# K loads from the fifth on issued by ScalarE instead of SyncE, in a grouped-query softmax attention kernel

## The chip, the cores and the metric

The kernel runs on one core of a Trainium2 chip. The core has TensorE (PE; PEld is its weight load), VectorE (DVE), ScalarE (ACT), GpSimd (POOL) and SyncE (SP), each with its own instruction stream, and 16 DMA engines that all transfers share. A DMA is started by an instruction in the stream of some engine and is carried out behind its back; its landing is told by a semaphore. The metric is the device time of one launch in microseconds (us).

## The reference

Attention without a mask, where four query heads share one head of K and V:

```python
B, Hq, Hkv, Sq, Sk, D = 16, 32, 8, 16, 2048, 128     # all bf16
scores = jnp.einsum("bhqd,bhkd->bhqk", q, k) * D ** -0.5   # k, v repeated 4 times along h
p = jax.nn.softmax(scores, axis=-1)
return jnp.einsum("bhqk,bhkd->bhqd", p, v)
```

There are 16 x 8 = 128 groups (one head of K and V each). A group has 4 x 16 = 64 query rows, 2048 keys, 512 KB of K and 512 KB of V. K and V together are 134 MB, each byte of which is used once.

## The kernel before

Two groups make a pair (128 query rows); there are NP = 64 pairs, called p. V is loaded a pair at a time (1 MB, into one of NV = 8 buffers). K is loaded two pairs at a time (2 MB, 32 loads, into one of NK = 3 buffers): K load n serves the pairs 2n and 2n+1. In HBM a partition's share is one run of 16 KB in a K load and two runs of 4 KB in a V load.

For every K load VectorE works two steps, one for each half of the keys. Step s = 2n + x handles half x of the keys for both pairs of load n:

- VectorE transposes the half of K into KT (line 562, two instructions, "kt" below), two steps ahead of its use. Each of the two adds 1 to the semaphore `sem_kt`, so a K load is used up when four have been added.
- TensorE multiplies it with the turned queries into S_ps (lines 376 and 406).
- VectorE scales S_ps into Sneg and keeps the row minimum (line 573); after the second half it forms the bias of the pairs' exponentials (line 582).

ScalarE then takes the exponential of one pair (line 674, into one of two P buffers). TensorE turns P (line 414), ScalarE copies it to SBUF (line 683), TensorE multiplies with V ("PV", lines 429, 483 and 489), and ScalarE, for the last five pairs VectorE, divides by the row sum (lines 697, 701, 655: "norm"). PV(p) waits for V load p; it runs in the round of exponential p + 4. GpSimd lays out the queries.

The order on TensorE and ScalarE is written out by hand (`pe_prog`, `act_prog`). ScalarE's order in a round p of the main loop is: norm of p - 4, exponential of p, two copies of pair p - 2, and, where p is even, a copy of turned queries (line 664). An exponential waits for the transposes of P of pair p - 2 (the buffer is shared), one of an even pair also for the bias.

All DMAs are issued by SyncE in one loop over t, which also sets their order:

```python
for t in range(NP + SLAG + 1):
    ...                                   # Q loads at fixed t
    if t < NP and t % 2 == 0:
        load_k(t // 2)                    # waits: sem_kt >= 4 * (n - NK) + 4
    if 0 <= t - VLAG < VLATE:
        load_v(t - VLAG)                  # waits: PV(p - 8) done
    if VLATE <= t - VLAG - 1 < NP:
        load_v(t - VLAG - 1)
    if 0 <= t - SLAG < NP:
        store(t - SLAG)                   # waits: norm of that pair done
```

With VLAG = 6 and SLAG = 14, K load n is followed by V load 2n - 6, the store of pair 2n - 14, V load 2n - 5 and the store of pair 2n - 13. From V load 50 on (VLATE) V stands one t later. SyncE handles these in order: a wait in front of K holds the V loads and stores behind it too. K load n waits until the transposes of K load n - 3 are done, since it goes into the same buffer.

Of the kernel before, what the change touches and what calls it, by code (L numbers as in the profile page):

```python
# [11 lines left out]
NK = 3  # L12
# [21 lines left out]
VBASE = 16  # L34
HEAD = 40
RING = 6
VLOOP = (3, 30)
VHEAD = 140
EXPBASE = 3
# [5 lines left out]
def both_heads(p, NP):  # L45
    return p < NP - NFAST and p % 2 == 0


def bass_standalone__gqa_softmax__sampling_kernel(
# [11 lines left out]
    NP = G // 2  # L61
    NQD = NP // 2
# [11 lines left out]
    Kn = [sb(f"Kn{i}", [128, 4 * J * 128], BF16) for i in range(NK)]  # L74
# [10 lines left out]
    Osb = [sb(f"O{i}", [128, 128], BF16) for i in range(NO)]  # L85
    nhalf = sb("nhalf", [128, 2, RING], F32)
    nbias = sb("nbias", [128, RING], F32)
    rowsum = sb("rowsum", [128, RING], F32)
    rrec = sb("rrec", [128, RING], F32)

    def col(x, p):
        return x[:, p % RING:p % RING + 1]

    def pair(x, Q):
        return x[:, 2 * Q % RING:2 * Q % RING + 2]

    def o_done(p):
        return sem_o[p // NOG % (NO // NOG)], 16 * NOG * (p // NO)
# [12 lines left out]
    sem_k = [sem(f"sem_k{i}") for i in range(NK)]  # L111
# [4 lines left out]
    sem_kt = sem("sem_kt")  # L116
# [19 lines left out]
    kf = k.rearrange("b h s d -> (b h s d)").rearrange("(n a x) -> n a x", n=NQD, a=128)  # L136
# [20 lines left out]
    def pt_slot(p):  # L157
        return p % 2 if p < 2 * M1 - 2 else p % NPT
# [75 lines left out]
    def stage_ap(op):  # L234
        return ST_ps[:, 512 * stage_of[op]:512 * (stage_of[op] + 1)]
# [4 lines left out]
    def o_ap(p):  # L240
        if p < NP - 4:
            return O_ps[:, 0:128]
        x = p - (NP - 4)
        return S_ps[:, 512 * x:512 * x + 128]
# [4 lines left out]
    def lay_part(eng, k):  # L249
# [4 lines left out]
        region = i if c < 2 else 0  # L254
        return eng.tensor_tensor(Q4[:, region, :, :, :], src, by, op=ALU.mult)  # L255

    with nc.Block() as block:

        @block.gpsimd
# [49 lines left out]

        @block.sync  # L310
        def _(sp):
            def load_k(n):
                s = n % NK
                if n >= NK:
                    sp.wait_ge(sem_kt, 4 * (n - NK) + 4)
                sp.dma_start(Kn[s][:, :], kf[n]).then_inc(sem_k[s], 16)  # L316

            def load_v(p):
                s = p % NV
                if p >= NV:  # L320
                    sp.wait_ge(sem_pv, p - NV + 1)
                if p < NP - 1:
                    dst = Vb[:, s, :, :, :].rearrange("a g j d -> a g (j d)")
                    sp.dma_start(dst, vf[:, 2 * p:2 * p + 2, :]).then_inc(sem_v[s], 16)
                    return
                for x, (lo, hi) in enumerate(LASTV):
                    dst = Vb[:, s, :, lo:hi, :].rearrange("a g j d -> a g (j d)")
                    src = vf[:, 2 * p:2 * p + 2, 128 * lo:128 * hi]
                    sp.dma_start(dst, src).then_inc(sem_vl[x], 16)

            def load_q(c):
                s = c % NQ
                if c >= NQ:
                    if c == 2:
                        sp.wait_ge(sem_qa, 4)
                    elif c == 3:
                        sp.wait_ge(sem_qb, 4)
                    else:
                        sp.wait_ge(sem_q4, Q4BASE + 4 * (c - NQ) - 4)
                src = qf[1024 * c:1024 * (c + 1), :].rearrange("(a j) d -> a j d", j=8)  # L340
                sp.dma_start(Qn[s][:, :, :], src).then_inc(sem_q[s], 16)

            def store(p):
                s = p % NO
                if p < NP - NLATE:
                    sp.wait_ge(sem_nm, NMBASE + p + 1)
                else:
                    sp.wait_ge(sem_nl, p - (NP - NLATE) + 1)
                sp.dma_start(of[128 * p:128 * (p + 1), :], Osb[s][:, :]).then_inc(o_done(p)[0], 16)  # L349

            for t in range(NP + SLAG + 1):
                if t == 4:
                    for s in range(NV):
                        sp.sem_inc(sem_v[s], VBASE)
                    sp.sem_inc(sem_nm, NMBASE)
                    sp.sem_inc(sem_exp, EXPBASE)
                for c in range(NQC):
                    if t == (QLOAD[c] if c < len(QLOAD) else 8 * c - QLEAD):
                        load_q(c)
                if t < NP and t % 2 == 0:  # L360
                    load_k(t // 2)
                if 0 <= t - VLAG < VLATE:
                    load_v(t - VLAG)
                if VLATE <= t - VLAG - 1 < NP:
                    load_v(t - VLAG - 1)
                if 0 <= t - SLAG < NP:
                    store(t - SLAG)
            for g in range(NO // NOG):
                sp.wait_ge(sem_o[g], 16 * NOG * len(range(g, NP // NOG, NO // NOG)))
# [187 lines left out]
        def _(dve):  # L557
            def kt(n, e, k_at=None):
                Q, x = divmod(n, 2)
                if x == 0 and e == 0:  # L560
                    dve.wait_ge(sem_k[Q % NK], 16 * (Q // NK + 1) if k_at is None else k_at)
                dve.transpose(  # L562
                    KT[n % NKT][:, :].rearrange("p (t b g e a) -> p e g t b a", t=J // 4, b=2, g=4, e=2)[:, e],
                    Kn[Q % NK][:, :].bitcast(F32).rearrange(
                        "p (g x t e b c) -> p x e g t b c", g=4, x=2, e=2, b=2, c=32)[:, x, e],
                ).then_inc(sem_kt, 1)
# [42 lines left out]
            for n in range(2):  # L609
                for e in range(2):  # L610
                    kt(n, e)
            V0, V1 = VLOOP
            assert (V1 - V0) % 3 == 0 and V0 % 3 == 0 and V1 < NQD
# [43 lines left out]
        @block.scalar  # L657
        def _(act):
            for op in act_prog:
                if op[0] == "qe":  # L660
                    k = op[1]
                    c, i = divmod(k, 4)
                    act.wait_ge(sem_stq, k + 1)
                    act.activation(  # L664
                        QT[c % 2][:, i // 2, :].rearrange("p (a x j) -> p x a j", x=2, j=4)[:, i % 2],
                        stage_ap(("Q", k)).rearrange("p (j a) -> p a j", j=4), ACT.Copy,
                    ).then_inc(sem_qe, 1)
                elif op[0] == "exp":
                    _, p = op
                    if p % 2 == 0:  # L670
                        act.wait_ge(sem_nb, p // 2 + 1)
                    if p >= 2 and (p % 2 == 1 or p <= 2 * M1 + 2):
                        act.wait_ge(sem_pt, 2 * p - 2)
                    act.activation(  # L674
                        P[p % 2][:, :].bitcast(BF16),
                        Sneg[p % NS][:, :], ACT.Exp,
                        bias=col(nbias, p), scale=-1.0, accum_out=col(rowsum, p),
                    ).then_inc(sem_exp, 1)
                elif op[0] == "pe":
                    _, p, h = op  # L680
                    act.wait_ge(sem_pt, 2 * p + h + 1)
                    slot = pt_slot(p)
                    act.activation(  # L683
                        PT[slot][:, 4 * h:4 * (h + 1), :].rearrange("p t q -> p (t q)"),
                        stage_ap(("PT", p, h)), ACT.Copy,
                    ).then_inc(sem_ev[h], 1 + (EVBASE if p == 0 else 0))
                else:
                    _, p = op
                    if p % 2 == 0 and (p < 2 * M1 - 4 or p == NP - NLATE - 1):
                        act.wait_ge(sem_rec, p // 2 + 1)  # L690
                    if p >= NO and p % NOG == 0:
                        act.wait_ge(*o_done(p))
                    act.wait_ge(sem_pv, p + 1)
                    if both_heads(p, NP):
                        for g in range(2):
                            rows = slice(64 * g, 64 * (g + 1))
                            ins = act.activation(Osb[p % NO][rows, :], O_ps[rows, 128 * g:128 * (g + 1)], ACT.Copy,  # L697
                                                 scale=col(rrec, p)[rows])
                        ins.then_inc(sem_nm, 1)
                        continue  # L700
                    act.activation(Osb[p % NO][:, :], o_ap(p), ACT.Copy,  # L701
                                   scale=col(rrec, p)).then_inc(sem_nm, 1)
# [28 lines left out]
```

## Time and profile before

| | |
|---|---|
| median of 3 runs | 339.35 us (338.94 to 339.59) |
| the profiled execution | 338.73 us |
| its span, first to last instruction | 336.9 us |
| busy share: PE, DVE, ACT, POOL | 89%, 90%, 73%, 21% |
| DMA | 138.60 MB, mean 411 GB/s |
| K loads, issue to landing (median) | 18.6 us |
| V loads, issue to landing (median) | 16.9 us |
| granted TensorE clock | 0.995 |

Busy shares are averages over the whole span. A wait names the instruction that ended it. "SPq" is SyncE's instruction queue: its DMA instructions are not work of an engine, but each takes time in the queue, and the next must wait for it. The time from issue to landing holds the time that a transfer stands behind others.

### The profile page before, as it was taken

How to read it: one execution, taken by the hardware profiler on the slowest of the kernel's cores; microseconds unless marked ns; L12 is line 12 of the kernel's file. 1: busy time of each engine (PE TensorE's matmuls, PEld its weight loads, DVE VectorE, ACT ScalarE, POOL GpSimd, SP SyncE). 2: the span in 40 equal slices, each digit the busy share in tenths (PEclk: the TensorE clock that was granted, in tenths of full speed). 3: DMA queues.
4: the chain of work that ended last, by engine and by line, in shares of the span. 5: the costliest groups of instructions: out<-in, count | busy, mean ns of one | idle time of the engine just before them, and what ended most of it. 6: DMA issues, size and time to landing. Idle time of an engine off the chain costs nothing.

```text
span 336.9 us, 7946 instructions
## 1 busy us (share of the span) xinstructions
PE 299.8 (89%) x3264; PEld 172.9 (51%) x2752; DVE 304.7 (90%) x457; ACT 245.9 (73%) x376; POOL 69.7 (21%) x64
## 2 busy tenths in 40 slices
PE   3466899999999999999998998889898879999885
PEld 3012456655566555665555456455465445555564
DVE  1788999999999999999998999989899999999941
ACT  3124887888888898888876877767867787877873
POOL 2802022221222222222122222022221200000000
PEclk9998999999999999999999999999999999999999
DMA  7999999999999999999999999999999999999996
GB/s 294 443 413 431 414 410 408 418 424 426 420 413 413 423 424 422 417 411 421 426 427 416 410 417 424 425 418 422 409 422 425 430 416 424 418 411 416 413 412 226
DMA packets 32670, 138.60 MB, mean 411 GB/s; under 512 B 10896, under 2 KB 11152, under 8 KB 28560
## 3 DMA queue, kind: packets, MB, share of 16 engines
q1 hardware_dynamic: 32656, 138.42, 100.6%
q8 instruction: 8, 0.13, 0.2%
q14 instruction: 6, 0.05, 0.0%
HBM read 136.31 MB, written 2.10 MB: 411 GB/s over the span
## 4 chain that ended last, share of the span: by engine, by line
DMA 39%; PE 32%; DVE 21%; ACT 3%; issue 2%; SPq 2%; DVEq 0%; ACTq 0%
DMA Kn<-in_k_dram 25%; DMA Vb<-in_v_dram 14%; DVE Sneg L573 11%; DVE KT L562 10%; PE O_ps L429 9%; PE S_ps L406 8%; PE S_ps L376 7%; PE ST_ps L414 6%; PE ST_ps L392 2%; ACT P L674 1%; SPq L349 1%; ACT PT L683 1%; ACT QT L664 0%; PE S_ps L489 0%; SPq L316 0%
## 5 line engine op out<-in xcount | busy, mean ns | idle before, releaser
L562 DVE STREAM_TRANSPOSE KT<-Kn 128x1024 f32<-128x1024 f32 x128 | 151.0, 1219 | 9.0 <-DMA Kn<-in_k_dram 9.0
L573 DVE TENSOR_SCALAR_CACHE_REDUCE Sneg<-S_ps 128x1024 f32<-128x1024 f32 x128 | 150.1, 1207 | 8.5 <-PE S_ps L376 8.4
L674 ACT ACTIVATE P<-Sneg,nbias 128x2048 bf16<-128x2048 f32 x64 | 128.1, 2002 | 31.7 <-DVE nbias L582 15.7
L255 POOL TENSOR_TENSOR Q<-Qn,mask 128x1024 bf16<-128x1024 bf16 x28 | 52.9, 1894 | 135.4 <-PE ST_ps L392 128.9
L429 PE MATMUL O_ps<-Vb,PT 128*64 (+1 forms) x1104 | 68.8, 238 | 11.3 <-DMA Vb<-in_v_dram 10.2
L406 PE MATMUL S_ps<-KT,Q 64*128 64x512 bf16 x384 | 74.8, 386 | 0.0
L376 PE MATMUL S_ps<-KT,Q 64*128 64x512 bf16 x384 | 74.2, 383 | 0.0
L429 PEld LDWEIGHTS O_ps<-Vb,PT 128*64 128x64 bf16 (+1 forms) x1104 | 55.6, 106 | 35.2 <-issue 27.9
L683 ACT ACTIVATE PT<-ST_ps 128x512 f32<-128x512 f32 x128 | 68.8, 590 | 3.0 <-PE ST_ps L414 2.2
L414 PE MATMUL ST_ps<-ident,P 128*128 128x128 f32 x512 | 68.2, 276 | 1.5 <-ACT PT L683 1.2
L414 PEld LDWEIGHTS ST_ps<-ident,P 128*128 128x128 f32 x512 | 56.3, 141 | 5.9 <-ACT P L674 2.2
L697 ACT ACTIVATE O<-O_ps,rrec 64x128 bf16<-64x128 f32 x56 | 20.3, 362 | 38.2 <-PE O_ps L429 30.9
L406 PEld LDWEIGHTS S_ps<-KT,Q 64*128 64x128 bf16 x384 | 18.6, 93 | 49.7 <-issue 38.2
L406 PE MATMUL S_ps<-KT,QT 64*128 64x512 bf16 x128 | 28.2, 423 | 13.5 <-DVE Sneg L573 9.8
L392 PEld LDWEIGHTS ST_ps<-ident,Q 128*128 128x128 f32 x128 | 15.2, 153 | 25.4 <-issue 25.4
L376 PE MATMUL S_ps<-KT,QT 64*128 64x512 bf16 x128 | 28.2, 422 | 0.0
L392 PE MATMUL ST_ps<-ident,Q 128*128 128x128 f32 x128 | 22.2, 306 | 6.6 <-DVE Q L605 5.4
L294 POOL COPY Q<-QT 128x512 int32<-128x512 int32 x24 | 14.6, 610 | 58.8 <-PE S_ps L376 58.8
L664 ACT ACTIVATE QT<-ST_ps 128x512 f32<-128x512 f32 x32 | 19.3, 603 | 9.8 <-PE ST_ps L392 9.8
L406 PEld LDWEIGHTS S_ps<-KT,QT 64*128 64x128 bf16 x128 | 7.7, 99 | 34.1 <-issue 29.5
L701 ACT ACTIVATE O<-O_ps,rrec 128x128 bf16<-128x128 f32 x31 | 11.7, 378 | 2.4 <-PE O_ps L489 2.3
L674 ACT ACTIVATION_READ_ACCUMULATOR P<-Sneg,nbias 128x1 f32 x64 | 12.0, 188 | 0.0
(25 smaller groups left out, 71.6 us busy)
## 6 DMA issues: line engine op xcount, KB each, us to landing
Kn<-in_k_dram SPq DMA_DIRECT2D x32, 2048.0 KB, 18.6
Vb<-in_v_dram SPq DMA_DIRECT2D x63, 1024.0 KB, 16.9
Qn<-in_q_dram SPq DMA_DIRECT2D x8, 256.0 KB, 14.7
out_dram<-O SPq DMA_DIRECT2D x64, 32.0 KB, 16.1
Vb<-in_v_dram SPq DMA_DIRECT2D x1, 768.0 KB, 12.8
Vb<-in_v_dram SPq DMA_DIRECT2D x1, 256.0 KB, 12.5
```

The source lines that it names most:

```text
L255: return eng.tensor_tensor(Q4[:, region, :, :, :], src, by, op=ALU.mult)
L376: return pe.add_instruction(mybir.InstMatmult(name=nc.get_next_instruction_name(), engine=mybir.EngineType.PE, ins=[pe.lower_ap(rhs), pe.l ...
L392: ins = pe.transpose(dst[:, 128 * j:128 * (j + 1)], src[:, j, :], ident4[:, :])
L406: ins = pe.matmul(s_ap, w, x, start=(acc == 0), stop=(acc == 3))
L414: ins = pe.transpose(dst[:, 128 * t:128 * (t + 1)], ptile[:, 128 * x:128 * (x + 1)], ident4[:, :])
L429: return pe.add_instruction(mybir.InstMatmult(name=nc.get_next_instruction_name(), engine=mybir.EngineType.PE, ins=[x, pe.lower_ap(w, for_ ...
L562: dve.transpose(KT[n % NKT][:, :].rearrange("p (t b g e a) -> p e g t b a", t=J // 4, b=2, g=4, e=2)[:, e], Kn[Q % NK][:, :].bitcast(F32). ...
L573: ins = dve.tensor_scalar(Sneg[p % NS][:, 1024 * x:1024 * (x + 1)].rearrange("p (t a m) -> p t a m", t=4, m=8), S_ps[:, 1024 * y:1024 * (y ...
L664: act.activation(QT[c % 2][:, i // 2, :].rearrange("p (a x j) -> p x a j", x=2, j=4)[:, i % 2], stage_ap(("Q", k)).rearrange("p (j a) -> p ...
L674: act.activation(P[p % 2][:, :].bitcast(BF16), Sneg[p % NS][:, :], ACT.Exp, bias=col(nbias, p), scale=-1.0, accum_out=col(rowsum, p),).the ...
L683: act.activation(PT[slot][:, 4 * h:4 * (h + 1), :].rearrange("p t q -> p (t q)"), stage_ap(("PT", p, h)), ACT.Copy,).then_inc(sem_ev[h], 1 ...
L697: ins = act.activation(Osb[p % NO][rows, :], O_ps[rows, 128 * g:128 * (g + 1)], ACT.Copy, scale=col(rrec, p)[rows])
```

## The change

The first four K loads (n = 0 to 3, NKSP = 4) stay where they are in SyncE's loop. The loads n = 4 to 31 leave it and are issued from ScalarE's stream, in front of the exponential of an odd pair p with n = (p + 7) / 2: load 4 before exponential 1, load 5 before exponential 3, and so on to load 31 before exponential 55. The wait in front of each is the same, `sem_kt >= 4 * (n - 3) + 4`, but it now stands in ScalarE's stream, between the norm of pair p - 4 and the exponential of pair p. V loads, Q loads and stores keep their order in SyncE's loop.

```diff
+NKSP = 4
...
+    def load_k(eng, n):
+        s = n % NK
+        if n >= NK:
+            eng.wait_ge(sem_kt, 4 * (n - NK) + 4)
+        eng.dma_start(Kn[s][:, :], kf[n]).then_inc(sem_k[s], 16)
+
...
         @block.sync
         def _(sp):
-            def load_k(n):
-                s = n % NK
-                if n >= NK:
-                    sp.wait_ge(sem_kt, 4 * (n - NK) + 4)
-                sp.dma_start(Kn[s][:, :], kf[n]).then_inc(sem_k[s], 16)
-
...
-                if t < NP and t % 2 == 0:
-                    load_k(t // 2)
+                if t % 2 == 0 and t // 2 < NKSP:
+                    load_k(sp, t // 2)
...
         @block.scalar
         def _(act):
             for op in act_prog:
+                if op[0] == "exp" and op[1] % 2 == 1 and NKSP <= (op[1] + 7) // 2 < NQD:
+                    load_k(act, (op[1] + 7) // 2)
```

## The prediction

> **What bounds the kernel now.** I read the head of the page first, then its part on DMA queues, then the DMA issues, the waits of the middle, SyncE's queue there, and last the chain of waits at the end.
>
> ```profile
> PE 299.8 (89%) x3264; PEld 172.9 (51%) x2752; DVE 304.7 (90%) x457; ACT 245.9 (73%) x376; POOL 69.7 (21%) x64
> ...
> DMA  7999999999999999999999999999999999999996
> ...
> q1 hardware_dynamic: 32656, 138.42, 100.6%
> ...
> Kn<-in_k_dram SPq DMA_DIRECT2D x32, 2048.0 KB, 18.6
> Vb<-in_v_dram SPq DMA_DIRECT2D x63, 1024.0 KB, 16.9
> ```
>
> The DMA engines are the bound: 9 in every slice between the ends, and packet times that add up to 100.6% of 16 engines' span. All of it is one queue, q1. VectorE and TensorE stand close behind at 90% and 89%. A K load takes 18.6 us to land, though its 2 MB need only 5.0 us of the engines (K load 30's landing less that of the store before it: 300.4 - 295.4, from the trace's landings); the rest is its place in the line. A V load, with its store, needs 2.55 us (landings 328.65 to 331.27 and their like).
>
> Waits between 165 and 290 us (engine, line, releaser: total us, times, longest):
>
> ```profile
> PE O_ps L429 <- DMA Vb<-in_v_dram: 10.2, 10, 1.6
> ACT P L674 <- PE ST_ps L414: 5.8, 11, 0.5
> DVE KT L562 <- DMA Kn<-in_k_dram: 5.3, 11, 0.9
> ```
>
> TensorE waits for V and VectorE for K, each for under 1.7 us at a time: both arrive just in time, in the one order that the single line gives them. The ACT row is the exponential of the odd pairs: 0.53 us each, always in front of the place where the K loads are to go.
>
> SyncE's queue (start, duration, instruction), and ScalarE at the same time:
>
> ```profile
> 180.90 1.22 SPq L316 DMA_DIRECT2D Kn<-in_k_dram  x1
> 182.16 0.44 SPq L324 DMA_DIRECT2D Vb<-in_v_dram  x1
> 182.64 6.55 SPq L349 DMA_DIRECT2D out_dram<-O  x1
> 189.23 0.60 SPq L324 DMA_DIRECT2D Vb<-in_v_dram  x1
> ```
> ```profile
> 189.50 0.38 ACT L701 ACTIVATE O<-O_ps,rrec 128x128 bf16<-128x128 f32 x1
> 190.41 2.00 ACT L674 ACTIVATE P<-Sneg,nbias 128x2048 bf16<-128x2048 f32 x1 [0.53 <-PE ST_ps L414]
> ```
>
> Issues that take 0.33 to 0.47 us early take up to 6.55 us here: the line is full and SyncE stands in it. The line holds some 5 to 8 MB (issued less moved, from the packet records).
>
> The chain at the end (start, us, what):
>
> ```profile
> 262.76 20.01 DMA Kn<-in_k_dram
> 282.80 2.37 DVE KT L562 x2
> ...
> 287.55 2.36 DVE KT L562 x2
> ...
> 296.91 2.37 DVE KT L562 x2
> ...
> 320.41 12.82 DMA Vb<-in_v_dram
> ```
>
> Up to 282.8 a K load sets the pace, then VectorE back to back, then the last V load. So the compute after 282.8 and the DMA both end at about 334 us; neither has room to spare.
>
> **The change part by part.** *SyncE loses 28 K issues and their waits.* SyncE waited 78.1 us in all for transposes in front of K, but 5.3 us of that between 165 and 290. As the DMA engines are never without work, the earlier V issues win nothing: the same 138.6 MB go through the same 16 engines. Worth 0. If that cover were gone (engines idle), an earlier V issue would count.
>
> *ScalarE gains 28 issues.* SyncE's shortest for K is 0.33 us, its median 0.43. In the loop it falls into the 0.53 us that the odd exponential waits anyway: 0. After the loop exponentials 53 and 55 have no idle time before them; 2 x 0.43 = 0.9 us at most, beside waits of 1.3 to 1.7 us that ScalarE has in front of the even norms there: 0 taken, 0.9 kept as an end. Its bound upward, if a full line held it as it holds SyncE, is a rival below.
>
> *The wait moved in front of the exponential.* Load n waits for the second transposes of step 2n - 5; these follow the bias of pairs 2n - 8 and 2n - 7 by 2.4 us (185.07 + 2.36 = 187.43 in one case), and exponential 2n - 7 starts at 190.41. So the wait is over 2.5 us before ScalarE arrives: 0. Behind it are queued the odd exponential, the copies of P and the next norm, and TensorE waits for those; none is held. But K is issued 0.5 us before the exponential, some 2.5 us after its buffer is free.
>
> *K gets its own line.* This is the part that moves time. K no longer stands behind V and stores; it shares the engines with them. The trace has no second bulk queue, so I bound K's share: all of the engines (2 MB in 5.0 us) or half (10.0 us). Either way it lands long before its need: in the trace, exponential 45 starts at 241.5 and the transposes of load 26 at 262.4, 20.8 us later. What K gets early V gets late, for the sum is fixed. Before, K load 29 landed at 290.2 (271.9 + 18.3), when 30 K and 51 V loads were in. PV(48), which needs 49 V loads, started at 279.2 with V load 48 there since 275.0. After the change, K load 29 goes out in front of exponential 51, 6.7 us before PV(48) (272.5 to 279.2), so when PV(48) wants V, 0.67 (half) to 1.0 (all) of load 29 has been moved. By the same byte clock, 49 V and 29.67 to 30 K loads are in at 290.2 - 2 x 2.55 - (0.33 to 0) x 5.0 = 283.4 to 285.1. PV(48) is then 4.2 to 5.9 us later than 279.2; I take 5.0, the middle, since no row speaks for either share.
>
> From there TensorE and ScalarE work at their own pace: exponentials 54 to 62 start from 288.0 to 325.8, 4.72 us each, hardly more than the 4.68 of the stretch around 140 us where nothing waits for DMA. So the lag is carried to the end, where V has now become early. At the end there is a little room: pair 63's last transposes finish at 331.1 and the multiplications of pairs 62 and 63 need 1.09 us each, so V apart the last norm could start at 333.3 instead of 334.49: 1.2 us.
>
> A page on arbitration bears on the share. The Trainium skill, "DMA: Bandwidth & Descriptors", section "Queues, rings and completion order", says that each DMA engine goes round the queues with work, a packet at a time. If a 16 KB run of K alternates with a 4 KB run of V, K would have about 80%, the lag would be near its upper end and the time some 0.6 us above my sum; no run here shows it yet.
>
> **Sum.** 5.0 - 1.2 = +3.8 us on the profiled execution: 338.73 (span 336.9 and 1.8 around it) + 3.8 = 342.5. That execution lies 0.6 under the median of the three runs, so 343.1. Its own ends: 4.2 - 1.2 = +3.0 and 5.9 - 1.2 + 0.9 = +5.6; if K is issued 3 us later than I think, 0.3 to 0.6 of a load less is ahead, which takes off up to 3 us: 340 to 345.
>
> **The rivals.**
> *No change.* DMA is the floor in both and the lag is caught up, as V comes at 2.55 us a pair after the last K. For it: 100.6%. Against: after 282.8 the pace is that of VectorE and TensorE. Time 339.4. The Trainium skill's same page, section "Issuing engines are not separate DMA queues", would have it so: issuing from several engines saves only the issue time. By that rule the time stays at 339.35. The trace agrees that SyncE's issue time is hidden, but not that order is free.
>
> *Two lines move bytes more slowly.* One row speaks for it: where an instruction fetch from another queue cuts into q1 (at 66.19 and 192.10 us, by packet records), the next two V packets take 0.27 to 0.38 us instead of 0.16, some 0.35 us lost on that engine. Once per K load that is 28 x 0.35 = 9.8 us on the floor: 353. For each of a load's 8 packets per engine it is 78 us: 421. Against: such a fetch goes elsewhere than to these buffers.
>
> *ScalarE is held by a full line* as SyncE is (up to 6.55 us). It has 0.5 us of wait there, about 0.9 us more behind it, and 10.3 - 9.36 us per K load that DMA leaves over (10.3: K landings 190.4 to 282.8 over nine loads; 9.36: the same where nothing waits for DMA, issues 92.75 to 102.11). Main-loop blocking is mostly absorbed, loads 30 and 31 are not: 2 x 2.4 (K's longest issue) = +4.8 on top: 348. Against: K's own line would hold three loads at most.
>
> *Faster: two lines fill each other's gaps.* A 4-byte packet takes 9 ns, so each packet has about 9 ns that move nothing; V's 16128 packets x 9 ns / 16 = 9 us. If a K packet runs in these gaps, the DMA floor and the lag both come earlier: 343.1 - 9 = 334. It decides from 4.5 us on (1.3% of the rate). The compute allows it: without DMA waits 31 double rounds of 9.36 us from exponential 1 (28.0) put exponential 63 at 318 instead of 328. Against: packets already follow each other without a break, and q1 moves 420 GB/s.
>
> **How the numbers follow.** V late, K early (343.1): 0.48. No change: 0.10. Slower lines: 0.14. ScalarE held: 0.10. Faster: 0.18. 0.2% (0.7 us) is about what a measurement can tell from nothing. So faster 0.18, same 0.10, slower 0.72. The range leaves out about half of the faster case below and two thirds of the slower lines above: 336.5 to 353.
>
> **What would show it.** DMA issues: K from ACT, landing in 5 to 13 us instead of 18.6. A second queue in the DMA part, the sum still near 100%. Waits 165 to 290: KT for K gone, O_ps for V clearly over 13 us. PV(48) 4 to 6 us later, exponentials 54 to 62 still 4.7 us apart, and DMA digits below 9 in the last slices. I would be wrong if K's issue on ACT took over 1 us, if GB/s in the middle moved from 419 by over 1%, or if exponential 54 still started by 288.

## The result and the profile after

The changed kernel takes 342.71 us (median of 5 runs, 342.20 to 344.56) against 339.35 us before: a ratio of 1.0106 (95% interval 1.0073 to 1.0139). A second series of the same kernel gave 343.19 us and 1.0116 (1.0090 to 1.0141). It is slower by some 3.4 us; 343.1 was forecast, in a range of 336.5 to 353. Ratios leave out runs more than 1.5% above the fastest of the same kernel; these are two, 346.28 and 347.97 us, of the first series of K one pair of rounds later.

From the page of the changed kernel, the parts on busy time, slices, DMA queues (packets, MB, share of 16 engines) and DMA issues:

```profile
PE 307.3 (90%) x3264; PEld 176.3 (51%) x2752; DVE 303.1 (88%) x457; ACT 246.1 (72%) x376; POOL 69.7 (20%) x64
...
DMA  7999999999999999999999999999999999999981
...
q1 hardware_dynamic: 28624, 79.70, 58.5%
q10 hardware_dynamic: 4032, 58.72, 40.3%
...
Vb<-in_v_dram SPq DMA_DIRECT2D x63, 1024.0 KB, 23.0
Kn<-in_k_dram ACTq DMA_DIRECT2D x28, 2048.0 KB, 10.4
```

K now has a queue of its own, q10. The two shares make 98.8% of a span of 342.7 us, where q1 alone had 100.6% of 336.9: the same work. A K load lands 10.4 us after its issue instead of 18.6, a V load 23.0 instead of 16.9. The DMA digits drop at the very end, where before only the last slice was below 9.

The same two stretches as windows (stretch, length, busy time of each engine, then granted clock, DMA share, GB/s), first of the kernel before, then of the changed one:

```profile
165.00:290.00 125.00, 112.46 (x1213) 64.56 (x1012) 116.76 (x174) 95.89 (x148) 25.03 (x20) 1.00 1.02 419
```
```profile
165.00:290.00 125.00, 115.68 (x1185) 66.96 (x988) 113.79 (x174) 93.27 (x146) 26.89 (x22) 0.96 1.02 420
334.00:343.00 9.00, 6.40 (x163) 5.72 (x158) 1.83 (x6) 5.21 (x8) 0.00 (x0) 1.00 0.11 24
```

The DMA engines move bytes as fast as before, 419 and 420 GB/s, and the first piece of the last V load lands at 333.9 us instead of 333.2 (the trace's landings). What is new is the stretch from 334 us on: DMA is done (share 0.11) and TensorE and ScalarE still work. The time went to compute that lags behind the data.

Where it fell behind, in the list of TensorE's instructions in time (start, us, instruction, idle time before it), and in the chain of waits of the changed kernel:

```profile
264.59 0.66 PE L393 MATMUL ST_ps<-ident,Q 128*128 128x128 f32 x4
267.57 1.41 PE L430 MATMUL O_ps<-Vb,PT 128*64 x32 [2.33 <-issue]
```
```profile
224.26 2.14 issue
226.41 1.23 PE O_ps L430 x32
...
265.24 2.33 issue
267.57 1.41 PE O_ps L430 x32
...
297.17 2.38 DVE Sneg L574 x4
...
338.49 1.93 PE S_ps L490 x64
```

TensorE stands for 2.33 us in front of PV(45). The profile calls it "issue", but V load 45 lands at 267.29 (issue 238.7 + 28.6) and the multiplication starts at 267.57: it is a wait for V. Such stops came at pairs 21, 29, 37 and 45, about 41 us apart; in the second profile of the change they came at pairs 21, 27, 31, 37 and 43, 21 to 31 us apart. After the last one no wait for DMA is in the chain: back-to-back VectorE, then TensorE to the end.

The lag can be read at one instruction, exponential 54, in ScalarE's list: before, after the change, and in the second series of the change.

```profile
288.02 2.00 ACT L674 ACTIVATE P<-Sneg,nbias 128x2048 bf16<-128x2048 f32 x1
```
```profile
295.79 2.00 ACT L677 ACTIVATE P<-Sneg,nbias 128x2048 bf16<-128x2048 f32 x1
```
```profile
293.58 2.00 ACT L677 ACTIVATE P<-Sneg,nbias 128x2048 bf16<-128x2048 f32 x1
```

It is 7.8 and 5.6 us late. From its start to the end of the span it is 336.9 - 288.0 = 48.9 us before, 342.7 - 295.8 = 46.9 and 340.4 - 293.6 = 46.8 in the two profiles of the change. So the kernel before had 2.0 us to spare behind exponential 54 (it waited for the last V loads), and the rest of the lag comes out as time: 5.8 and 3.5 us. The first profile of the change is that of its slowest run (344.56), the second of its fastest (342.24).

### The profile page after: what moved, and what is told of

It is laid out like the page before. It is cut to its first block, busy times and chain, and to the rows that moved or that the text cites. A ratio compares the mean times of both kernels' runs of the same rounds, so it can differ in the third digit from the quotient of the medians.

```text
span 342.7 us, 7946 instructions
## 1 busy us (share of the span) xinstructions
PE 307.3 (90%) x3264; PEld 176.3 (51%) x2752; DVE 303.1 (88%) x457; ACT 246.1 (72%) x376; POOL 69.7 (20%) x64
## 4 chain that ended last, share of the span: by engine, by line
PE 72%; DVE 12%; DMA 8%; issue 5%; ACT 2%; SPq 0%; ACTq 0%; DVEq 0%
PE O_ps L430 18%; PE S_ps L407 17%; PE ST_ps L415 15%; PE S_ps L377 15%; DVE Sneg L574 7%; DMA Vb<-in_v_dram 6%; DVE KT L563 4%; PE ST_ps L393 4%; DMA Kn<-in_k_dram 2%; PE O_ps L490 2%; PE S_ps L490 1%; PE O_ps L484 1%; ACT P L677 1%; ACT PT L686 1%; ACT QT L667 0%
## 5 line engine op out<-in xcount | busy, mean ns | idle before, releaser
L430 PE MATMUL O_ps<-Vb,PT 128*64 (+1 forms) x1104 | 69.5, 239 | 11.3 <-issue 9.8
L407 PE MATMUL S_ps<-KT,Q 64*128 64x512 bf16 x384 | 76.2, 393 | 0.0
L377 PE MATMUL S_ps<-KT,Q 64*128 64x512 bf16 x384 | 75.3, 389 | 0.0
L415 PE MATMUL ST_ps<-ident,P 128*128 128x128 f32 x512 | 71.6, 285 | 1.8 <-ACT PT L686 1.2
L415 PEld LDWEIGHTS ST_ps<-ident,P 128*128 128x128 f32 x512 | 59.0, 146 | 6.4 <-ACT P L677 2.6
L407 PE MATMUL S_ps<-KT,QT 64*128 64x512 bf16 x128 | 28.9, 437 | 12.8 <-DVE Sneg L574 9.4
L377 PE MATMUL S_ps<-KT,QT 64*128 64x512 bf16 x128 | 29.1, 438 | 0.0
## 6 DMA issues: line engine op xcount, KB each, us to landing
Kn<-in_k_dram ACTq DMA_DIRECT2D x28, 2048.0 KB, 10.4
```

What stands on the lines that cost most here:

```text
L377: return pe.add_instruction(mybir.InstMatmult(name=nc.get_next_instruction_name(), engine=mybir.EngineType.PE, ins=[pe.lower_ap(rhs), pe.l ...
L407: ins = pe.matmul(s_ap, w, x, start=(acc == 0), stop=(acc == 3))
L415: ins = pe.transpose(dst[:, 128 * t:128 * (t + 1)], ptile[:, 128 * x:128 * (x + 1)], ident4[:, :])
L430: return pe.add_instruction(mybir.InstMatmult(name=nc.get_next_instruction_name(), engine=mybir.EngineType.PE, ins=[x, pe.lower_ap(w, for_ ...
```

## The experiments

The theory under test ("order theory"): the DMA engines move the same bytes at the same rate, but K's own queue lets K run ahead by about one load, V is late by as much, and the compute cannot make up the lag before the end. The rivals: a K load issued by ScalarE, or carried by a second queue, costs time wherever it stands ("queue theory"); or the loss is made at the start, where load 4 is late and the clock low ("head theory").

All in one table; exponential 54, the first piece of the last V load and the span are those of each profiled execution, in us. A profiled execution can lie at an end of its runs: those of six back and of V from 30 on are the fastest of theirs, that of half a pair later is the second fastest, that of V throughout the slowest.

| kernel | ratio to before (95%) | exp 54 | last V | span | span - exp 54 |
|---|---|---|---|---|---|
| before | | 288.0 | 333.2 | 336.9 | 48.9 |
| the change | 1.0106 (1.0073 to 1.0139) | 295.8 | 333.9 | 342.7 | 46.9 |
| the change again | 1.0116 (1.0090 to 1.0141) | 293.6 | 333.7 | 340.4 | 46.8 |
| only the last six on ScalarE | 1.0242 (1.0219 to 1.0266) | 298.3 | 333.3 | 345.1 | 46.8 |
| the last six back on SyncE | 1.0080 (1.0051 to 1.0109) | 290.9 | 333.7 | 337.8 | 46.9 |
| the last twelve back on SyncE | 0.9998 (0.9985 to 1.0011) | 287.7 | 333.6 | 337.9 | 50.2 |
| half a pair of rounds later | 1.0036 (1.0012 to 1.0060) | 290.5 | 333.9 | 337.4 | 46.9 |
| one pair of rounds later, again | 1.0089 (1.0064 to 1.0114) | 290.5 | 333.3 | 341.5 | 51.0 |
| one queue, V two places later from 30 | 1.0073 (1.0052 to 1.0095) | 292.8 | 333.3 | 339.7 | 46.9 |
| one queue, V two places later throughout | 1.0218 (1.0196 to 1.0240) | 299.1 | 339.7 | 346.2 | 47.1 |

**Only the last six K loads on ScalarE.**

```diff
-NKSP = 4
+NKSP = 26
```

> Only the last six K loads (26 to 31) go out from ScalarE; loads 0 to 25 stay with SyncE. Order theory: what counts is the lead of K at the last loads, so most of the loss is there: PV waits for V between about 255 and 290 us, exponential 54 4 to 7 us after 288, time 341.5 to 343.5 us. Queue theory: 6 of 28 loads, so 339.4 + 0.7 = 340.1 us. Head theory: 339.4 us.

Measured 347.28 us (346.59 to 348.35): more than the full change costs, with 6 of 28 loads. Neither the queue theory, which gave 340.1, nor the head theory, which gave 339.4, can make such a time; the order theory had the direction but too little. The trace shows why: in the list of K issues, load 25 from SyncE (at 231.3 us) and load 26 from ScalarE (at 240.4 us), with their times to landing.

```profile
L262 SPq DMA_DIRECT2D Kn<-in_k_dram x1: 2218/2218/2218, 231.3 to 231.3; - x1
...
DMA to landing us min/median/max: 25.8/25.8/25.8
```
```profile
L262 ACTq DMA_DIRECT2D Kn<-in_k_dram x1: 378/378/378, 240.4 to 240.4; - x1
...
DMA to landing us min/median/max: 11.0/11.0/11.0
```
```profile
264.67 3.53 PE L430 MATMUL O_ps<-Vb,PT 128*128 x16 [8.44 <-issue]
```

Load 25 stands in SyncE's line behind V and needs 25.8 us; load 26, issued 9 us later, goes past it and past the V loads 43 to 45 and is in at 251.4, 22 us before its transposes start at 273.4; load 27 is in at 263.7, 19 us before its use. V load 44 lands at 264.47 instead of 254.79, and TensorE stands 8.44 us in front of PV(44) (the third fence). The change of queue in mid-run puts two K loads ahead of V at once, not one: 28 K loads are in with V load 44, where the kernel before had 26. The change itself also had K two loads ahead at its last stop, but that stop fell on PV(45), whose V load the kernel before had 2.9 us before its use (257.35 and 260.24); PV(44) followed its V load by 0.2 us (254.79 and 255.03). That may be why six loads cost more than 28; it was not tested.

**The last six, and the last twelve, back on SyncE.** Loads 4 to 25, or 4 to 19, go out from ScalarE, the others from SyncE's loop as before.

```diff
+NKBACK = 26        # second kernel: 20
...
-                if t % 2 == 0 and t // 2 < NKSP:
+                if t < NP and t % 2 == 0 and not NKSP <= t // 2 < NKBACK:
...
-                if op[0] == "exp" and op[1] % 2 == 1 and NKSP <= (op[1] + 7) // 2 < NQD:
+                if op[0] == "exp" and op[1] % 2 == 1 and NKSP <= (op[1] + 7) // 2 < NKBACK:
```

> The complement: loads 4 to 25 go out from ScalarE, the last six from SyncE's loop as before. Order theory: in the middle V is late by the same 5 to 7 us as after the change, but the last K loads stand behind V again, V catches up before the end, exponential 54 near 288 to 291, time 339 to 341 us. Queue theory: 22 of 28 loads, 339.4 + 2.6 = 342.0 us. Head theory: 342.7 us.

> K loads 4 to 19 go out from ScalarE, 20 to 31 from SyncE's loop as before. Order theory: V is late by 4 to 7 us up to about load 20; after that K stands behind V again, and as the compute needs 4.68 us a pair where DMA needs 5.15, some 0.47 us a pair is caught up over the last 24 pairs: exponential 54 at 288 to 290, time 339 to 340.5 us. Queue theory: 16 of 28 loads, 339.1 + 1.9 = 341.0 us.

With six back: 341.64 us (339.66 to 343.90), above the 339 to 341 of the order theory and near the 342.0 of the queue theory, so this run alone does not tell them apart. With twelve back: 339.39 us (338.98 to 339.79), a ratio of 0.9998, although 16 of 28 loads still go out from ScalarE; the queue theory gave 341.0. Its head is that of the change too, with the same loads on ScalarE up to load 19, so the loss is not made there either. A lag made in the middle is paid back if there are enough pairs left, and six loads are too few. The chain of waits with twelve back (start, us, what) is that of the kernel before again: a K load, VectorE, the last V load.

```profile
262.47 19.80 DMA Kn<-in_k_dram
282.30 2.37 DVE KT L564 x2
...
320.16 13.47 DMA Vb<-in_v_dram
```

**One queue, K further ahead of V.** Nothing is issued by ScalarE; V stands later in SyncE's loop. First throughout:

```diff
-VLAG = 6
+VLAG = 8
```

> The kernel before, all loads from SyncE in one queue, but each V load two places later in SyncE's loop (VLAG 8 instead of 6), so that K is one load further ahead of V. Order theory: the same loss as by the change, without a second queue and without an issue by ScalarE: waits of PV for V well above the 13.9 us of before, K transposes wait for nothing, exponential 54 some 4 to 7 us after 288, the last V load lands at 333 to 334 as before, time 341.5 to 344.5 us. Queue theory and head theory: 339.4 us, as before.

Measured 346.67 us, more than expected, and the last V load landed at 339.7 and not at 333 to 334. The window of the start shows why the experiment is not clean: with V held back from the first load on, the DMA engines ran out of work there (share 0.88, 351 GB/s, where the kernel before has 1.01 and 422).

```profile
9.00:42.00 33.00, 21.47 (x124) 7.11 (x80) 27.68 (x37) 11.12 (x14) 9.34 (x5) 0.95 0.88 351
```

So the same from V load 30 on, with the start left alone:

```diff
-VLATE = 50
+VLATE = 30
...
-                if VLATE <= t - VLAG - 1 < NP:
-                    load_v(t - VLAG - 1)
+                if VLATE <= t - VLAG - 2 < NP:
+                    load_v(t - VLAG - 2)
```

> The kernel before, one queue, nothing issued by ScalarE, and the start unchanged; from V load 30 on each V load stands two places later in SyncE's loop (before: one place, from load 50 on), so that K is one load further ahead of V from there. Order theory: V late by one K load, 5 us; PV waits for V grow past 13.9 us, K transposes wait for nothing after load 20, exponential 54 at 291 to 294, the last V load still lands at 333 to 334, time 341.5 to 345 us. Queue theory (ScalarE or the second queue costs): 339.1 us.

Measured 341.91 us (341.57 to 342.52), 1.0073: two thirds of the loss, with one queue and no issue by ScalarE. Its waits between 165 and 290 us (engine, line, releaser: us, times, longest):

```profile
PE O_ps L429 <- DMA Vb<-in_v_dram: 13.1, 8, 6.6
DVE KT L562 <- DMA Kn<-in_k_dram: 1.2, 2, 0.8
```

VectorE hardly waits for K any more (5.3 us before), TensorE waits for V for up to 6.6 us at a time (1.6 before), and exponential 54 starts at 292.8, 4.8 us late.

**K later, still from ScalarE.** The load's place moves by half a pair of rounds, or by one.

```diff
-                if op[0] == "exp" and op[1] % 2 == 1 and NKSP <= (op[1] + 7) // 2 < NQD:
-                    load_k(act, (op[1] + 7) // 2)
+                if op[0] == "exp" and op[1] % 2 == 0 and NKSP <= (op[1] + 6) // 2 < NQD:
+                    load_k(act, (op[1] + 6) // 2)
```

> All K loads from 4 on from ScalarE, half a pair of rounds later: load n in front of exponential 2n - 6. Order theory: K's lead falls from 10 us to some 5 us without landing late, so V is late by 2 to 4 us instead of 5 to 7.5, time 340 to 342 us, waits on K under 2 us. Queue theory: 342.7 us, as for any 28 loads on ScalarE.

Measured 340.35 us (338.94 to 342.69), 1.0036 (1.0012 to 1.0060): all 28 loads still on ScalarE, and two thirds of the loss gone. This takes back part of K's lead by itself, the number of issues, their engine and their queue unchanged. The spread is wide, and the order theory's 340 to 342 holds it. For the second kernel "+ 5" stands for "+ 7" (odd pairs):

> K from load 4 on still goes out from ScalarE, but one pair of rounds later: load n in front of exponential 2n - 5 instead of 2n - 7. Order theory (the loss is that K is a load early and V a load late, carried to the end): K loses its lead of some 10 us and lands just in time, V is no longer late; exponential 54 starts near 288 to 290 instead of 295.8, waits of the K transposes for DMA come back (over 4 us in all), and the time is 338.5 to 341 us. If K then lands late by itself (10.4 us of landing in 10.3 us per load), it may stay up to 343, with the waits on K and not on V. Queue theory (a K load issued by ScalarE on a second queue costs, wherever it stands): 342.7 us. Head theory (load 4 is late and shares with V at the start): load 4 is later still, so 342.7 us or more.

> The kernel of the first experiment again (load n in front of exponential 2n - 5), for a profile of an undisturbed execution. In the seven other profiles the end is the start of exponential 54 plus 46.8 to 47.1 us wherever neither K nor V holds up the last pairs. Order theory: K now waits on the exponentials by itself (10.4 us of landing right before its use), so K transposes wait for DMA 4 us or more after 165 us, and the last loads come late: exponential 54 at 288 to 292, and the end 1 to 6 us later than exponential 54 plus 46.9. Time 341 to 344 us. Queue theory: exponential 54 near 294 to 296 as after the change, no waits on K, and the end 46.9 us later.

The first series gave a ratio of 1.0099 (1.0069 to 1.0128), the second 1.0089 (342.96 us). The time did not fall to 338.5 to 341. In the profile of the second series the loss stands on both: two stops for V are left, 2.0 us at PV(35) and 2.4 us at PV(45), and exponential 54 is 2.4 us late; behind it K holds up the end. VectorE waits for K for 4.2 us in all after 165 us. VectorE's list in the second series, the instructions that a K load released at the end:

```profile
284.89 2.37 DVE L563 STREAM_TRANSPOSE KT<-Kn 128x1024 f32<-128x1024 f32 x2 [0.49 <-DMA Kn<-in_k_dram]
305.08 2.37 DVE L563 STREAM_TRANSPOSE KT<-Kn 128x1024 f32<-128x1024 f32 x2 [0.77 <-DMA Kn<-in_k_dram]
316.15 2.37 DVE L563 STREAM_TRANSPOSE KT<-Kn 128x1024 f32<-128x1024 f32 x2 [1.61 <-DMA Kn<-in_k_dram]
```

Load 31 comes in at 316.1 instead of 310.5, and the end is 51.0 us after exponential 54. Too early starves V, too late starves K; of the three places tried on ScalarE the middle one is the best.

**The change a second time.**

> The change itself a second time, for a second profile. Order theory: K lands 10 to 12 us after its issue and some 10 us before its use, TensorE stops for V about once in eight pairs for about 4 us, exponential 54 at 292 to 296 depending on where the last stop fell, last V load at 333 to 334, time 342 to 344.5 us. If instead the low granted clock in the first 42 us (0.69 in the first profile of the change, 0.95 before) made the loss, a profile with 0.9 or more there ends within 1 us of the kernel before.

Measured 343.19 us. In its profile the clock between 9 and 42 us was 0.95, as before the change; exponential 54 is still 5.6 us late and the span 3.5 us longer. The low clock of the first profile's start (0.69) is therefore not the cause. The stops came every four to six pairs here and not every eight, as was expected from the first profile.

No version beat the kernel before; the one with twelve back equals it.

## Why the prediction was right

**The DMA floor and the earlier V issues: right.** "The same 138.6 MB go through the same 16 engines": 419 against 420 GB/s, and the last V load in at 333.2 against 333.7 to 333.9. The rivals of slower lines (353) and of filled gaps (334) are out by these numbers. The Trainium skill, "DMA: Bandwidth & Descriptors", section "Issuing engines are not separate DMA queues", has all DMAs run on the same 16 engines, and by these rates the trace agrees; its step from there to a gain in issue time alone is what fails here, since the order of arrival changes.

**ScalarE's issues: right.** SyncE's list and ScalarE's list at the same time:

```profile
67.26 7.01 SPq L350 DMA_DIRECT2D out_dram<-O  x1
```
```profile
67.70 0.33 ACTq L262 DMA_DIRECT2D Kn<-in_k_dram  x1
```

While SyncE stands for 7.01 us in its full line, ScalarE issues K in 0.33 us. So the rival in which a full line holds ScalarE (348) is out. The issue costs nothing, though it doesn't fall where it was put, into the wait of the odd exponential. It runs from 206.63 to 206.96 us, beside the norm before that, and goes out 1.0 us before the exponential and not 0.5; the wait stays at 0.53 us:

```profile
206.63 0.33 ACTq L262 DMA_DIRECT2D Kn<-in_k_dram  x1
206.73 0.38 ACT L704 ACTIVATE O<-O_ps,rrec 128x128 bf16<-128x128 f32 x1
207.64 2.00 ACT L677 ACTIVATE P<-Sneg,nbias 128x2048 bf16<-128x2048 f32 x1 [0.53 <-PE ST_ps L415]
```

**K early, V late: right in kind, with two terms mis-sized.** The sum took 2 MB of K to be moved within 5.0 us (all of the engines) or 10.0 us (half) from the issue. The packet records show another course. For load 22, issued at 206.63, the DMA queues from 206.7 to 210.1 us and from 210.2 to 216.4 us (queue: packets, MB, share of 16 engines):

```profile
q1 hardware_dynamic: 532, 1.39, 102.4%
q10 hardware_dynamic: 5, 0.00, 0.1%
```
```profile
q10 hardware_dynamic: 136, 2.03, 77.1%
q1 hardware_dynamic: 229, 0.54, 22.0%
```

At first K's queue moves nothing (0.00 MB); then it takes 77% of the engines. In the 24 of the 28 loads whose packets stand clear of the load before, the first packet moves 3.5 us after the issue, the packets take 6.3 us and the landing follows 0.6 us later (medians). So the landing of 10.4 us, which looks like half of the engines, is a wait and then most of the engines. The 3.5 us were put at nothing in the sum: of a load issued 6.7 us before PV(48), some (6.7 - 3.5) / 6.3 = 0.5 would have been moved (an estimate), outside the bounds of 0.67 to 1.0.

The lag at the end came out at 5.6 and 7.8 us where the sum had 5.0, and the spare time behind exponential 54 at 2.0 us where it had 1.2. These errors cancel in part: the net is 3.5 and 5.8 us in the two profiles and 3.4 between the medians; the sum said 3.8. That 343.1 came so near is partly luck.

**The place of the wait: wrong.** The lag was worked out at PV(48), "when PV(48) wants V". In neither profile did PV(48) wait. The last long stop was at PV(45) in the first and at PV(43) in the second, and the byte clock has to be read there. For the first: 46 V and 28 K loads had landed at 267.3, which by the landings before (load 27 at 272.5 with 48 V loads in) is 272.5 - 2 x 2.55 = 267.4. It was the right clock at the wrong pair; at PV(45), which started at 260.2 before, it gives 267.4 - 260.2 = 7.2 us. K was two loads ahead there: when V load 45 landed before the change, at 257.35, 26 K loads were in. At PV(48) V was no longer late. The sum had K load 29 go out at 272.5, at the time of the kernel before; but the stop at PV(45) held up ScalarE too, the load went out at 279.4, and V load 48 was in at 280.0 and not at 283.4 to 285.1.

**The share by packets: borne out.** Read with one run of 16 KB as a packet, the rule of the same page of the Trainium skill, section "Queues, rings and completion order", gave K 80% of the engines; that a run is a packet was my reading. By that 2 MB take some 2.10 MB / (0.8 x 420 GB/s) = 6.2 us, an estimate. The trace agrees: K's packets took 6.3 us, and while they moved, 2436 packets of K went with 2419 data packets of the other queue in these 24 loads, one for one. That the lag would therefore be near its upper end did not follow, because of the 3.5 us before the first packet. (By the sum's own clock this share moves all of load 29 in 6.7 us, which is 0.9 us above the middle and not 0.6.)

**What should have shown it.** K from ACT landing in 5 to 13 us, a second queue with the sum near 100%, no waits on K, exponentials 54 to 62 4.7 us apart (295.8 to 333.2 is 4.68 each) and low digits at the end all came. PV(48) was 7.8 and 5.6 us later (4 to 6 were forecast). The row "O_ps for V over 13 us" did not come: between 165 and 290 us TensorE's stops for V, in part listed as "issue", add up to 6.9 and 11.2 us in the two profiles, against 10.2 before. TensorE hardly waited longer for V in the middle; it waited in fewer, longer stops, and the lag of the last one was still there at the end.

## What to carry to other kernels

Where the DMA engines are full from end to end, as here, a second issuing queue added no bandwidth (419 and 420 GB/s); it dealt out the same bandwidth in another order, and the stream that was served early was paid for by the one that came late. Before such a change, count at the tightest wait which loads each order has delivered by then, and how much compute is left after the last load. A lag costs nothing while DMA sets the pace and much if it is still there when the loads end: with twelve of the K loads left in the old order it cost nothing, with six it did.

## What the runs showed of the hardware that was not expected

Two queues, one with 16 KB packets and one with packets of 4 KB and less, did not share the engines evenly by bytes: it was one packet for one, and the queue with the large packets had 77% of the bytes while it moved. From its issue a 2 MB load still took 10.3 to 12.0 us, since 3.5 us went by before its first packet (3.46 to 3.67 in 24 loads); why is open. The limit of a queue's line is its own: SyncE's issues stood up to 7.95 us while ScalarE's 28 took 0.33 to 0.44 us each.

V did not come evenly late. As long as the compute runs, K goes out every 9.36 us and gets its bytes, while the K and V loads of two pairs need 10.3 us of the engines; V is short of the difference, some 0.9 us each time. When V's lead is used up, TensorE stops once and ScalarE with it. The next K load goes out late (load 27 in at 267.3, load 28 issued at 269.0), and V catches up (loads 45, 46 and 47 at 267.3, 269.9 and 272.5). From stop to stop the two profiles need 5.0 to 5.3 us a pair, which is the pace of the DMA. The stops and these times are in the trace; that they come about in this way was not tested. Where the last stop falls may also be why the change's runs spread over 2.4 us and those with six back over 4.2, where the kernel before has 1.4 to 1.9 in its series; this too was not tested.
